# Four 512-token expert items as straight code with the scatter in place, item tables laid over the partitions, one loop left for 64-token items

## The chip, the cores and the metric

The kernel runs on one core of a Trainium2 chip. The metric is the device time of one execution in microseconds; the time of a kernel is the median of several runs. Before the change it is 1185.59 us, the median of 3 runs between 1184.55 and 1185.77.

## What is computed

Three layers follow each other: attention between 8 batches of 512 tokens and 32 state rows, a mixture of 8 experts of which each token takes at most one, and a dense layer with a gated hinge. Cut to what matters:

```python
def _moe_ref(x, w_skip, w_gate, w1, w2):            # x: 4352 x 512
    do_compute = x @ w_skip > 0
    out = x.copy()
    xc = x[do_compute]
    logits = xc @ w_gate
    e_idx = np.argmax(logits, axis=1)
    gate_w = softmax(logits)[np.arange(len(xc)), e_idx]
    for e in range(8):                               # w1[e]: 512x1024, w2[e]: 1024x512
        y[e_idx == e] = gate_w * (relu(xc[e_idx == e] @ w1[e]) @ w2[e])
    out[do_compute] = xc + y

def _moe2_ref(x, w_in, w_out):                       # 512x2048, 2048x512
    h = x @ w_in
    return (h * np.clip(h + 3.0, 0.0, 6.0) / 6.0) @ w_out
```

With the inputs of the runs 2720 tokens are computed. The experts have 544, 0, 0, 32, 544, 1024, 512 and 64 of them: five full blocks of 512 tokens and four remainders of at most 64. These counts are known only when the kernel runs.

## The kernel before, in words

All matmuls on wide data are made in three passes on a high and a low part of each operand (`PAIRS`); the parts come from a ScalarE cast and a VectorE subtraction (`split`, L799, used by `split1` for w1 and `split2` for w2 of an expert).

**Attention** runs over the 8 batches in an order written out by hand (`STEP` and its variants), leaves its rows in `x_in` and scatters the rows that go to an expert into `xs`, sorted by expert, by indirect transfers of GpSimd (`scat`, L379).

**The plan** (`plan`, L593) turns the counts into tables. An item is a block of 512 rows of one expert (an A item) or one of up to 64 rows (a B item). `items_a` (L634, 24 small VectorE operations) writes `tab_a`: how often the A loop runs, and expert and first row of each A item. `items_b` (L668, 21 operations, six of them on 544 columns: 68 possible items times 8 experts) writes `tab_b` and `lim`, the same for the B items. Everywhere the item lies along the free axis.

**The first A item** (`first`, L947) is straight code, for an expert that has 512 rows early. For f of 0 to 7 it runs `s1a(f)`, 12 matmuls 128x512 into `ph`, and `s2a(f-1)`, 12 matmuls into the four sums `po`. Between them it works off a list in small portions (`some`): the last tokens' routing, the plan, and three **conversions** of the last layer's weights (`kept(1)` to `kept(3)`, NEARLY = 4; one is made within attention). A conversion turns two 512 KB blocks of 8-byte numbers into float parts in nine steps (`Weights.cut`, L1264) and stores them (`keep`, L1341). At f = 7 `turn_and_s2a` (L907) transposes the next item's 512 rows (`turn`, 4 groups of 4 transposes into two PSUM banks of the tag `tr`) between the halves of `s2a(6)`. At the end `out_a` (L918) multiplies the four sums by the gates and adds the rows kept in `xr` (`keep`, L931, ScalarE copies).

**The A loop** (`item_a`, L1009, `For_i` at L1144) then runs four times, since `tab_a` holds the larger of the number of A items left and (16-4)/3 = 4. One pass scatters the rows of the item before (`scatter_a`, L922), computes an A item like `first`, computes one B item between its matmuls (`item_b`, L1076, advanced by `next(small)` at the f in SMALL_AT), makes three conversions (`Convert`), and fetches the next item's weights, rows and high and low parts, in the last pass too. `take_wait` (L940) is a one-column GpSimd operation ahead of each scatter.

**The B loop** (L1162) takes the B items that are left, two at a time; with these inputs there are none, and it is passed over. Each loop ends for all engines together (semaphores and drains that the trace puts down to L1144, L1162 and L1851). After it, at L1171 to L1176, come the last A item's four scatters, the reading back of four converted blocks (`again`, `again2`) and their preparation (`W.early`).

**The last layer** (`ffn`, L1358) begins with `fetch(0, True)` and `fetch(2, True)`, four loads of 256 KB of `x_in` on SyncE's queue, which wait for the scatters; the 16 transposes of L1413 and the first matmuls of `stage_a` (L1482) follow. SyncE issues nearly all transfers, in program order.

## Time and profile before

| what | us |
|---|---|
| median of 3 runs | 1185.59 |
| the profiled execution | 1177.61 |
| its span, first to last instruction | 1175.9 |
| TensorE busy in the span | 1110.4 (94%) |
| VectorE busy | 848.4 (72%) |
| ScalarE busy | 499.3 (42%) |
| GpSimd busy | 110.6 (9%) |
| from the first matmul of the last layer to the end | 732.2 |

The profile is of one execution. The span counts the instructions; 1.71 us lie around it. A row of the timeline gives start, length, engine, line, operation, what it writes and reads, and in brackets how long the engine had stood idle and what ended that. Matmuls are pipelined, so consecutive rows overlap by some tenths of a us: 12 matmuls follow each other every 2.80 us though a row reads 2.96. TensorE's granted clock is given as a share of its full 2.4 GHz.

### The profile page before, as it was taken

The numbers are of one execution on the slowest core, as the hardware profiler recorded it, in microseconds if no ns is written. First come the engines' busy times: TensorE is split into PE (matmuls) and PEld (weight loads), VectorE is DVE, ScalarE is ACT, GpSimd is POOL, SyncE is SP. The second block draws the span as 40 slices with busy tenths as digits, with TensorE's granted clock in tenths as the row PEclk, the third lists the DMA queues.
The fourth block names the chain that finished last, engine by engine and source line by source line (L and its number), as shares of the span: only waits on it lengthen the run. The fifth ranks groups of instructions, "written<-read, shape, count | busy, mean of one in ns | idle before, by whom it ended". The sixth has DMA issues, their size and how long they took to land.

```text
span 1175.9 us, 17522 instructions
## 1 busy us (share of the span) xinstructions
PE 1110.4 (94%) x5991; PEld 920.5 (78%) x5991; DVE 848.4 (72%) x1659; ACT 499.3 (42%) x954; POOL 110.6 (9%) x167
## 2 busy tenths in 40 slices
PE   7898979999999919999999999999999999999998
PEld 4555756676767617888998989999889999899997
DVE  6879896666766635686788768876887778876776
ACT  7786443444444414454433343334333343334331
POOL 5466301020201010000000000000000000000000
PEclk9899998999999968999999999999999999999999
DMA  6875888787878746984554256416552454334532
GB/s 199 288 260 200 297 296 300 259 294 265 312 254 305 257 173 256 350 319 175 178 198 152 109 187 212 155 43 226 204 177 86 178 177 173 135 116 164 195 134 90
DMA packets 93080, 245.39 MB, mean 209 GB/s; under 512 B 13744, under 2 KB 43056, under 8 KB 87376
## 3 DMA queue, kind: packets, MB, share of 16 engines
q1 hardware_dynamic: 88496, 233.28, 56.6%
q0 software_dynamic: 4512, 11.17, 2.5%
q8 instruction: 42, 0.69, 0.2%
q14 instruction: 30, 0.25, 0.1%
HBM read 184.75 MB, written 63.22 MB: 211 GB/s over the span
## 4 chain that ended last, share of the span: by engine, by line
PE 61%; DMA 1%; DVE 1%; ACT 0%; issue 0%; POOL 0%; POOLq 0%; SPq 0%; ACTq 0%
PE o L1636 28%; PE b L1584 24%; PE o L1502 4%; PE b L1482 4%; PE o L1413 1%; DMA x_in_dram<-xr,toks 1%; DMA raw<-x_in_dram 0%; ACT g L1306 0%; PE b L1413 0%; DVE cv L1427 0%; POOL x_in_dram L765 0%; DVE g L1307 0%; DVE c L1598 0%; DVE cv L1598 0%; POOL seen L942 0%
## 5 line engine op out<-in xcount | busy, mean ns | idle before, releaser
L1636 PE MATMUL o<-wo,g 128*128 128x512 f32 x1440 | 334.3, 390 | 0.0
L1636 PEld LDWEIGHTS o<-wo,g 128*128 128x128 f32 x1440 | 269.7, 188 | 54.7
L1584 PE MATMUL b<-xc,wc 128*128 128x384 f32 x1680 | 299.6, 335 | 1.6 <-ACT c L1608 1.6
L1584 PEld LDWEIGHTS b<-xc,wc 128*128 128x128 f32 x1680 | 292.2, 188 | 4.0 <-ACT c L1608 1.9
L1307 DVE TENSOR_TENSOR g<-cv,g 128x384 fp32r<-128x384 f32 x160 | 89.3, 558 | 92.8 <-ACT g L1306 92.8
L1306 ACT CAST g<-cv 128x384 fp32r<-128x384 f32 x160 | 82.2, 514 | 157.1 <-DVE cv L1427 157.1
L902 PE MATMUL po<-w2p,hT 128*128 128x512 f32 x480 | 123.1, 403 | 0.0
L890 PE MATMUL ph<-xTa,w1p 128*128 128x512 f32 x480 | 120.3, 401 | 1.1 <-ACT w1p L801 0.8
L902 PEld LDWEIGHTS po<-w2p,hT 128*128 128x128 f32 x480 | 88.3, 190 | 31.3 <-issue 5.5
L1426 ACT ACTIVATE cv<-cv,three 128x384 f32<-128x384 f32 x80 | 49.2, 615 | 143.4 <-DVE cv L1598 135.8
L890 PEld LDWEIGHTS ph<-xTa,w1p 128*128 128x128 f32 x480 | 90.6, 190 | 23.5 <-ACT w1p L801 1.2
L1598 DVE TENSOR_TENSOR c<-b,c 128x384 f32<-128x384 f32 x160 | 87.1, 551 | 16.8 <-PE b L1584 16.4
L1645 DVE SCALAR_TENSOR_TENSOR hl<-o,hl 128x512 f32<-128x512 f32 x140 | 92.7, 683 | 2.1 <-PE o L1636 2.0
L895 DVE SCALAR_TENSOR_TENSOR hT<-ph,hT 128x512 fp32r<-128x512 f32 x40 | 27.5, 689 | 48.7 <-ACT hT L894 48.5
L1426 ACT ACTIVATE cv<-c,three 128x384 f32<-128x384 f32 x80 | 49.2, 614 | 15.0 <-DVE g L1307 15.0
L1598 DVE TENSOR_TENSOR cv<-b,cv 128x384 f32<-128x384 f32 x80 | 44.3, 554 | 14.6 <-PE b L1584 13.4
L894 ACT ACTIVATE hT<-ph 128x512 fp32r<-128x512 f32 x40 | 23.8, 596 | 70.3 <-PE ph L890 64.4
L279 PE MATMUL pxr<-BD,AT 128*128 128x265 f32 x128 | 40.9, 435 | 10.5 <-DVE AT L242 5.2
L1427 DVE SCALAR_TENSOR_TENSOR cv<-cv,c 128x384 f32<-128x384 f32 x80 | 44.1, 552 | 5.8 <-ACT cv L1426 4.8
L1645 DVE SCALAR_TENSOR_TENSOR acc<-o,acc 128x512 f32<-128x512 f32 x70 | 44.8, 681 | 1.3 <-PE o L1636 1.3
L1427 DVE SCALAR_TENSOR_TENSOR cv<-cv,cv 128x384 f32<-128x384 f32 x80 | 43.9, 549 | 0.0
L1608 ACT COPY c<-b 128x384 f32<-128x384 f32 x40 | 19.2, 481 | 55.1 <-PE b L1584 54.9
(294 smaller groups left out, 1302.7 us busy)
## 6 DMA issues: line engine op xcount, KB each, us to landing
wc<-wc SPq DMA_DIRECT2D x36, 1792.0 KB, 6.8
wo<-wo SPq DMA_DIRECT2D x37, 1024.0 KB, 4.9
raw<-in_moe_w_dram SPq DMA_DIRECT2D x48, 512.0 KB, 10.6
spare<-in_moe_w_dram SPq DMA_DIRECT2D x35, 512.0 KB, 4.9
raw<-in_moe_w_in_dram SPq DMA_DIRECT2D x16, 512.0 KB, 6.7
raw<-in_moe_w_out_dram SPq DMA_DIRECT2D x16, 512.0 KB, 5.4
x_in_dram<-XR SPq DMA_DIRECT2D x8, 1024.0 KB
wo<-hl SPq DMA_DIRECT2D x16, 512.0 KB, 7.7
```

What stands on the lines that cost most here:

```text
L890: nc.tensor.matmul(ph, lhsT=w1p[a][:, f, kk, :], rhs=xTa[b][:, kk, :], start=(n == 0), stop=(n == 11))
L902: nc.tensor.matmul(po[c], lhsT=hp[f][a][:, P * c:P * c + P], rhs=w2p[b][:, f, :], start=(f == 0 and n == 0), stop=(f == NF - 1 and n == 2),)
L1306: nc.scalar.copy(hi, src)
L1307: nc.vector.tensor_tensor(lo, src, hi.bitcast(F32), op=ALU.subtract)
L1426: nc.scalar.activation(gg, h, AF.Relu, bias=k["three"])
L1427: nc.vector.scalar_tensor_tensor(gg, gg, 6.0, h, op0=ALU.min, op1=ALU.mult)
L1482: nc.tensor.matmul(ph, lhsT=w1(f, a, kk), rhs=xt[b][:, kk, :], start=(n == 0), stop=(n == 11))
L1502: nc.tensor.matmul(pos[c], lhsT=gg[a][:, P * c:P * c + P], rhs=w2(f, b), start=(f == 0 and n == 0), stop=(f == NFF - 1 and n == 2),)
L1584: nc.tensor.matmul(t, lhsT=w[:, s:s + P], rhs=XC[m // NP][:, x, b, kk, :], start=(i == 0), stop=(i == 5))
L1598: v.tensor_tensor(c, t, u, op=ALU.add)
L1636: nc.tensor.matmul(po, lhsT=gs[f][a][:, o:o + P], rhs=w[:, DM * (2 * f + b):DM * (2 * f + b) + DM], start=(q == 0), stop=(q == 5),)
L1645: nc.vector.scalar_tensor_tensor(dst, po, 1.0 / 6.0, dst, op0=ALU.mult, op1=ALU.add)
```

## The change

The four A items that always ran become straight code, NA = 4, in `for i in range(1, NA + 1)`; full blocks beyond them would be cut into B items. `end_a` takes the place of `turn_and_s2a` for the last two f, of `out_a`, `scatter_a` and `keep`: it ends the sums one by one, multiplies each into the row tile itself and scatters it at once. Two row tiles alternate (`xn`). The last A item fetches, splits and transposes nothing for a next one. Of the last layer's weights two instead of four blocks are converted by the end of `first` (NEARLY = 2); the four items make 3, 3, 3 and 5 conversions in a steady trickle (`convert`), each block loaded during the one before it. SMALL_AT now counts half steps, before and after `s2a`. The plan has the item on the partition: 26 small operations, then three transposes and four VectorE operations (`second`), which run at the end of `first`. The four loads of `x_in` for the last layer are issued after the A items and again in each pass of the B loop.

```diff
-NA = B * TB // 512 + 2
-NB = 8 * NE + 4
+NA = 4
+NSMALL = B * TB // 64 + NE + 2
...
+    n, end, c2, r, nb = (new(nm, [NE]) for nm in ("n", "end", "c2", "r", "nb"))
+    t, m = new("t", [NE, 8]), new("m", [NE + 1, NE])
+    ends, G, w, Z, red = k["ends"], k["G"], new("w", [3, NE]), new("Z", [5, NE]), new("red", [5])
...
+        lambda: v.tensor_scalar(Z[:, 0:2], both, k["item"], None, op0=ALU.is_le),
+        lambda: v.tensor_tensor(w, G[:, :, 1:], G[:, :, 0:NE], op=ALU.subtract),
+        lambda: v.tensor_tensor(Z[:, 2:4], Z[:, 0:2], w[:, 0:2], op=ALU.mult),
+        lambda: v.tensor_tensor(Z[:, 4], Z[:, 1], w[:, 2], op=ALU.mult),
+        lambda: v.tensor_reduce(red, Z, axis=AX.X, op=ALU.add),
+        lambda: v.tensor_scalar(tab[:, 0:2], red[:, 0:2], 7.0, None, op0=ALU.min),
+        lambda: v.tensor_tensor(red[:, 2:5], red[:, 2:5], G[:, :, 0], op=ALU.add),
+        lambda: v.tensor_scalar(tab[:, 2:4], red[:, 2:4], float(NSLOT), None, op0=ALU.min),
+        lambda: v.tensor_scalar(red[:, 4:5], red[:, 4:5], k["item_q"], None, op0=ALU.subtract),
...
+    def second():
+        pt = k["turned"]()
+        vals = [red[:, 4:5], red[:, 1:2], red[:, 3:4]]
+        lim, tb = k["lim"], k["tab_b"]
+        def turn(i):
+            nc.tensor.transpose(pt[:, i, :], vals[i].to_broadcast([P, P]), k["ident"])
+        return [
+            lambda: [turn(i) for i in range(3)],
+            lambda: v.tensor_copy(lim, pt[:, 0, 0:NSMALL]),
+            lambda: v.tensor_scalar(tb[:, 0, :], pt[0:1, 1, 0:NSMALL], 7.0, None, op0=ALU.min),
+            lambda: v.tensor_scalar(tb[:, 1, :], pt[0:1, 2, 0:NSMALL], float(NSLOT), None, op0=ALU.min),
+            lambda: v.tensor_scalar(k["nb"], eb[0:1, 8:9], float(NA), None, op0=ALU.max),
+        ]
...
-        def turn_and_s2a(po, f):
-            if f < NF - 2:
-                return s2a(po, f)
-            self.turn(0)
-            self.turn(1)
-            s2a(po, f, (0, 1))
-            self.turn(2)
-            s2a(po, f, (2, 3))
-            self.turn(3)
-        def out_a(po):
-            for c in range(4):
-                gated(xr[:, c, 0:DM], po[c], xr[:, c])
-        def scatter_a():
-            for c in range(4):
-                take_wait(xr[:, c])
-                i = self.scatter(xr[:, c, 0:DM], toks[:, c:c + 1])
-                tc.declare_no_dep(i, group="xo", reason="rows of different tokens")
-                tc.add_to_no_dep_group("xo", i)
+        def end_a(po, i, last):
+            x, tok = xn[i % 2], toks[:, 4 * (i % 2):4 * (i % 2) + 4]
+            nc.vector.tensor_copy(tok, x[:, :, DM + 1])
+            if last:
+                s2a(po, NF - 2, (0,))
+            else:
+                self.turn(0, (i + 1) % 2)
+                self.turn(1, (i + 1) % 2)
+                s2a(po, NF - 2, (0, 1))
+                self.turn(2, (i + 1) % 2)
+                s2a(po, NF - 2, (2, 3))
+                self.turn(3, (i + 1) % 2)
+            for c in range(4):
+                if last and c < 3:
+                    s2a(po, NF - 2, (c + 1,))
+                s2a(po, NF - 1, (c,))
+                gated(x[:, c, 0:DM], po[c], x[:, c])
+                take_wait(x[:, c])
+                ins = self.scatter(x[:, c, 0:DM], tok[:, c:c + 1])
+                tc.declare_no_dep(ins, group="xo", reason="rows of different tokens")
+                tc.add_to_no_dep_group("xo", ins)
...
+        def convert():
+            todo = list(range(NEARLY, NFF))
+            raw = {todo[0]: self.W.load(todo[0])}
+            for i, f in enumerate(todo):
+                parts, steps = self.W.cut(raw.pop(f))
+                for n, step in enumerate(steps):
+                    step()
+                    if n == 4 and i + 1 < len(todo):
+                        raw[todo[i + 1]] = self.W.load(todo[i + 1])
+                    if n == len(steps) - 1:
+                        self.W.keep(f, parts)
+                    yield
...
-                    self.fetchx(row_a(0))
+                    self.fetchx(row_a(0), xn[1])
...
-                if f >= 1:
-                    turn_and_s2a(po, f - 1)
+                if f == 6:
+                    fetch_b(row_b(0), xb[0])
+                    b0 = expert_b(0)
+                    for c in range(3):
+                        fetch_w(b0, c, chunks[c])
+                if 1 <= f < NF - 1:
+                    s2a(po, f - 1)
                 if f >= 5:
                     split1(2 * f - 10)
                     split1(2 * f - 9)
-            s2a(po, NF - 1)
             some(999)
+            for step in k["tables"]():
+                step()
+            end_a(po, 0, False)
             split1(6)
             split1(7)
-            out_a(po)
...
+        def item_a(i, conv):
+            more = i < NA
+            if more:
+                en, rn = expert_a(i), row_a(i)
+            small = item_b(i - 1, chunks, h32, xb[0], x32[0], hs, yb[0], 0, 1 if more else 0)
+            if more:
+                for f in range(0, NF, 2):
+                    self.fetch1(en, f)
+            po = accs()
+            steps = 9 * CONVERTED[i - 1]
+            done = 0
+            for f in range(NF):
+                if f == 0:
+                    next(small)
+                split2(f)
+                if f % 2 and more:
+                    self.fetch2(en, f - 1)
+                s1a(f)
+                for _ in range(SMALL_AT.count(2 * f)):
+                    next(small)
+                if f == 5 and more:
+                    self.fetchx(rn, xn[(i + 1) % 2])
+                while done < steps * (f + 1) // (NF - 1) and done < steps:
+                    next(conv)
+                    done += 1
+                if 1 <= f < NF - 1:
+                    s2a(po, f - 1)
+                for _ in range(SMALL_AT.count(2 * f + 1)):
+                    next(small)
+                if more and f >= 1:
+                    split1(f - 1)
+            if not more:
+                for f in range(4):
+                    self.W.again(f, self.W.room(f // 2))
+                for f in range(2):
+                    self.W.again2(f)
+            end_a(po, i, not more)
+            if more:
+                split1(NF - 1)
...
-        na = nc.values_load(tab_a[0:1, 0:1], min_val=0, max_val=B * TB // 512)
-        nb = nc.values_load(tab_b[0:1, 0:1], min_val=0, max_val=8 * NE)
-        fetch_b(row_b(0), xb[0])
-        e0 = expert_b(0)
-        for c in range(3):
-            fetch_w(e0, c, chunks[c])
-        with tc.For_i(0, na, 1, iteration_sync="reg_based") as i:
-            item_a(i)
+        nb = nc.values_load(k["nb"][0:1, 0:1], min_val=0, max_val=NSMALL)
+        conv = convert()
+        for i in range(1, NA + 1):
+            item_a(i, conv)
+        self.W.early()
+        self.W.x_first(self.x_in)
...
-        with tc.For_i(na, nb, 2, iteration_sync="reg_based") as i:
+        with tc.For_i(NA, nb, 2, iteration_sync="reg_based") as i:
             for u in range(2):
...
-        scatter_a()
-        for f in range(4):
-            self.W.again(f, self.W.room(f // 2))
-        for f in range(2):
-            self.W.again2(f)
-        self.W.early()
+            self.W.fetch_first(self.x_in)
...
-NEARLY = 4
-NCONV = 3
-LOAD_AT = (0, 0, 3)
-CONV_AT = (1, 3, 5)
-STORE_AT = (3, 5, 7)
-SMALL_AT = (2, 2, 3, 4, 5, 5, 6, 6, 7)
+NEARLY = 2
+CONVERTED = (3, 3, 3, 5)
+SMALL_AT = (2, 4, 5, 7, 9, 11, 12, 13, 14)
...
+    def x_first(self, x_in):
+        self.x0 = [self.scratch(0).bitcast(F32).rearrange("p (c f) -> p c f", c=2) for _ in range(2)]
+        self.fetch_first(x_in)
+    def fetch_first(self, x_in):
+        rows = x_in[0:S].rearrange("(p c) f -> p c f", c=4)
+        for c in range(4):
+            self.tc.nc.sync.dma_start(self.x0[c // 2][:, c % 2], rows[:, c])
...
-    fetch(0, True)
-    fetch(2, True)
+    xw[0], xw[2] = W.x0
```

Where it moves instructions, three places. **VectorE at the end of the first A item**: `w1p`, `w2p` are parts of weights, `hT` of the hidden layer, `xTa` of the transposed rows, `xr`/`xn` the row tiles. Before:

```order
L679 TENSOR_REDUCE tb<-room 128x68
L685 TENSOR_TENSOR spare<-room,ws 128x544
L686 TENSOR_REDUCE lim<-spare 128x68
L687 TENSOR_TENSOR room<-room,w 128x544
L688 TENSOR_REDUCE pr<-room 128x68
L802 TENSOR_TENSOR w1p_1888<-raw_0_97,w1p_1887 128x512 x2
L802 TENSOR_TENSOR w2p_1890<-raw_2029,w2p_1889 128x512
L895 SCALAR_TENSOR_TENSOR hT<-ph,hT 128x512
L802 TENSOR_TENSOR xTa_1747<-ptx,xTa_1746 128x4x128 x4
L802 TENSOR_TENSOR w1p_1888<-raw_1_98,w1p_1887 128x512 x4
L938 SCALAR_TENSOR_TENSOR xr<-po_1946,xr 128x512
```

and with the change:

```order
L762 TENSOR_TENSOR w2p_1896<-raw_2029,w2p_1895 128x512
L854 SCALAR_TENSOR_TENSOR hT<-ph,hT 128x512
L762 TENSOR_TENSOR w1p_1894<-raw_1_98,w1p_1893 128x512 x2
L656 COPY lim<-ptt 128x78
L657 TENSOR_SCALAR tab_b<-ptt 1x78
L658 TENSOR_SCALAR tab_b<-ptt 1x78
L659 TENSOR_SCALAR nb<-ends 1x1
L869 CAST toks<-xn 128x4
L762 TENSOR_TENSOR xTa_1753<-ptx,xTa_1752 128x4x128 x4
L891 SCALAR_TENSOR_TENSOR xn<-po_1952,xn 128x512
```

The wide table operations are gone from between the parts of the weights; four narrow ones that read a PSUM bank of the tag `tr` (`ptt`) stand between `hT` of f = 7 and the row parts `xTa`. **TensorE at the same place**, with the change:

```order
L652 MATMUL ptt<-ident,red 128x128 x3
L768 MATMUL ptx<-ident,xr 128x128 x4
L768 MATMUL ptx<-ident,xr 128x128 x4
```

Ahead of the row transposes, which stood there alone before, three table transposes take one of the two `tr` banks. **SyncE at the end of the A items**, before, from the end of the A loop:

```order
L1144 COMPARE_AND_BRANCH
L1144 UNCONDITIONAL_BRANCH
L1162 COMPARE_AND_BRANCH
L1162 UNCONDITIONAL_BRANCH
L1350 DMA cv_3210<-w 128x512
L1355 DMA hl<-wo 128x1024 x2
L1395 DMA raw_3263<-x_in_dram 128x512 x2
L1395 DMA raw_3266<-x_in_dram 128x512 x2
L1350 DMA wf<-w 128x512
```

and with the change:

```order
L1312 DMA cv_4231<-w 128x512
L1317 DMA hl<-wo 128x1024 x2
L1213 DMA raw_4303<-x_in_dram 128x512 x2
L1213 DMA raw_4304<-x_in_dram 128x512 x2
L1112 COMPARE_AND_BRANCH
L1112 UNCONDITIONAL_BRANCH
L1312 DMA wf<-w 128x512
```

One loop's branches are gone; the other's now stand behind the four loads of `x_in` instead of ahead of the scatters that these wait for.

## Rows read from the trace of the kernel before

**Rows 1.** Windows: stretch, length; busy PE, PEld, DVE, ACT, POOL; clock; DMA share; GB/s.

```profile
125.79:184.52 58.73, 49.35 (x221) 38.53 (x220) 50.97 (x127) 25.84 (x48) 8.64 (x10) 0.94 0.77 276
184.52:243.48 58.96, 57.91 (x263) 41.98 (x263) 37.05 (x64) 24.39 (x44) 6.01 (x10) 0.97 0.83 280
243.48:300.82 57.34, 56.29 (x263) 40.80 (x262) 37.79 (x65) 24.30 (x44) 6.05 (x10) 1.00 0.83 282
...
415.68:443.70 28.02, 3.79 (x16) 2.99 (x16) 8.59 (x16) 4.71 (x8) 5.49 (x8) 0.54 0.53 185
443.70:1175.90 732.20, 726.10 (x3624) 647.23 (x3624) 538.93 (x1006) 278.51 (x512) 0.00 (x0) 1.00 0.48 175
```

**Rows 2.** Timeline of TensorE at the end of the first A item.

```profile
160.04 2.96 PE L902 MATMUL po<-w2p,hT 128*128 128x512 f32 x12
163.78 0.73 PE L890 MATMUL ph<-xTa,w1p 128*128 128x512 f32 x2 [0.79 <-ACT w1p L801]
...
167.26 1.03 PE L808 MATMUL ptx<-ident,xn 128*128 128x128 f32 x8
...
176.09 1.11 PE L808 MATMUL ptx<-ident,xn 128*128 128x128 f32 x4 [6.39 <-DVE xTa L802]
...
184.52 0.41 PE L1051 MATMUL ptx<-ident,xb 128*128 128x128 f32 x2 [1.87 <-DVE xr L938]
184.75 7.36 PE L890 MATMUL ph<-xTa,w1p 128*128 128x512 f32 x24
```

**Rows 3.** Timeline of VectorE in the same place: first and last table operation, rows after.

```profile
163.97 0.23 DVE L674 TENSOR_SCALAR eb<-end 128x8 f32<-128x8 f32 x1
...
175.21 0.23 DVE L699 TENSOR_TENSOR lim<-lim,tb 128x68 f32<-128x68 f32 x1
175.35 1.28 DVE L802 TENSOR_TENSOR xTa<-ptx,xTa 128x512 fp32r<-128x512 f32 x2
```

**Rows 4.** Windows of the tile `cv` alone: busy time of VectorE and ScalarE, three conversions.

```profile
125.79:184.52 58.73, 16.69 (x27) 1.82 (x3) 0.94 0.77 276
```

**Rows 5.** Timeline of TensorE in the A loop: end of the last pass, one wait within.

```profile
392.16 1.08 PE L1117 MATMUL pob<-spare 128*64 128x256 f32 x8 [0.79 <-ACT spare L1052]
...
407.62 0.66 PE L808 MATMUL ptx<-ident,xn 128*128 128x128 f32 x4
408.54 0.66 PE L808 MATMUL ptx<-ident,xn 128*128 128x128 f32 x4 [0.26 <-DVE xTb L1123]
408.95 1.65 PE L902 MATMUL po<-w2p,hT 128*128 128x512 f32 x6
...
412.28 0.60 PE L808 MATMUL ptx<-ident,xn 128*128 128x128 f32 x4
412.64 3.04 PE L902 MATMUL po<-w2p,hT 128*128 128x512 f32 x12
```

**Rows 6.** DMA issues by tile: count, KB each, median us from issue to landing.

```profile
raw<-in_moe_w_dram SPq DMA_DIRECT2D x48, 512.0 KB, 10.6
...
raw<-in_moe_w_out_dram SPq DMA_DIRECT2D x16, 512.0 KB, 5.4
```

**Rows 7.** Timeline from the A loop's end to the last layer, VectorE and GpSimd.

```profile
415.35 2.72 DVE L938 SCALAR_TENSOR_TENSOR xr<-po,xr 128x512 f32<-128x512 f32 x4
...
424.21 0.18 POOL L942 TENSOR_TENSOR seen<-xr 128x1 f32<-128x1 f32 x1 [13.85 <-DMA x_in_dram<-xr,toks]
425.08 1.00 POOL L765 DMA_INDIRECT x_in_dram<-xr,toks  x1 [0.69 <-issue]
```

**Rows 8.** Queue instructions around the passed-over loop: count, ns min/median/max, first and last start.

```profile
L1162 PEldq COMPARE_BRANCH  x2: 73/1706/3340, 419.8 to 420.0; - x2
L1851 SPq EVENT_SEMAPHORE  x2: 17/17/17, 418.8 to 423.9; - x2
```

**Rows 9.** The chain that ended last, in order of time: start, length, what.

```profile
429.73 6.24 DMA x_in_dram<-xr,toks
...
439.24 3.81 PE o L1413 x16
```

More of the change, by code (lines that the diff above doesn't have):

```diff
@@ L586, with plan @@
 NXS = NSLOT + 640
-NA = B * TB // 512 + 2
-NB = 8 * NE + 4
+NA = 4
+NSMALL = B * TB // 64 + NE + 2
 Q = 64
-def plan(tc, sp, c, early, k, spare):
+ROUND = 1.5 * 2.0 ** 23
+def plan(tc, sp, c, early, k):
     nc = tc.nc
@@ L632, in plan @@
-    tab = k["tab_a"]
-    rows, js = new("rows", [NA])[0:1], new("js", [NA])
-    items_a = [
+    n, end, c2, r, nb = (new(nm, [NE]) for nm in ("n", "end", "c2", "r", "nb"))
+    t, m = new("t", [NE, 8]), new("m", [NE + 1, NE])
+    ends, G, w, Z, red = k["ends"], k["G"], new("w", [3, NE]), new("Z", [5, NE]), new("red", [5])
+    ea, eb = ends[:, 0:9], ends[:, 10:19]
+    tab = k["tab"]
+    both = ends[:, 1:19].rearrange("p (i e) -> p i e", i=2)[:, :, 0:NE]
+    first = [
         lambda: v.scalar_tensor_tensor(c2, early, -512.0, c, op0=ALU.mult, op1=ALU.add),
@@ L636, in plan @@
         lambda: v.tensor_tensor(t, over(c2, 8), under(k["i512"], NE), op=ALU.is_ge),
-        lambda: v.tensor_reduce(n[:, 0:8], t, axis=AX.X, op=ALU.add),
-        lambda: v.scalar_tensor_tensor(r, n[:, 0:8], -512.0, c2, op0=ALU.mult, op1=ALU.add),
-        lambda: v.tensor_tensor(t, over(r, 8), under(k["iq"], NE), op=ALU.is_gt),
-        lambda: v.tensor_reduce(n[:, 8:16], t, axis=AX.X, op=ALU.add),
-        lambda: v.tensor_tensor(m, under(n, 16), k["low16"], op=ALU.mult),
-        lambda: v.tensor_reduce(end, m, axis=AX.X, op=ALU.add),
@@ L645, in plan @@
-        lambda: v.tensor_scalar(js, k["iota"][:, 0:NA], end[:, 7:8], None, op0=ALU.min),
-        lambda: v.tensor_tensor(ps, over(js, 16), under(end, NA), op=ALU.is_ge),
-        lambda: v.scalar_tensor_tensor(base, early, 512.0, k["base"], op0=ALU.mult, op1=ALU.add),
-        lambda: v.tensor_reduce(ta[:, 0, :], ps, axis=AX.X, op=ALU.add),
-        lambda: v.scalar_tensor_tensor(g[:, 1:8], end[:, 0:7], -512.0, base[:, 1:], op0=ALU.mult, op1=ALU.add),
-        lambda: v.scalar_tensor_tensor(ta[:, 0, :], ps[:, :, 7], -8.0, ta[:, 0, :], op0=ALU.mult, op1=ALU.add),
@@ new lines, in plan @@
+        lambda: v.tensor_reduce(n, t, axis=AX.X, op=ALU.add),
+        lambda: v.tensor_tensor(m[:, 0:NE], under(n, NE), k["low"][:, 0:NE], op=ALU.mult),
+        lambda: v.tensor_reduce(end, m[:, 0:NE], axis=AX.X, op=ALU.add),
+        lambda: v.tensor_scalar(ea[:, 1:], end, float(NA), None, op0=ALU.min),
+        lambda: v.scalar_tensor_tensor(G[:, 0, 0:NE], early, 512.0, k["base_a"], op0=ALU.mult, op1=ALU.add),
+        lambda: v.tensor_tensor(n, ea[:, 1:], ea[:, 0:NE], op=ALU.subtract),
+        lambda: v.scalar_tensor_tensor(G[:, 0], ea, -512.0, G[:, 0], op0=ALU.mult, op1=ALU.add),
@@ L700, in items_b @@
         ]
-    return items_a, items_b
+    return first, second
 class Experts:
@@ L782, in loadx @@
         row = self.value(self.tab_e, 1, NSLOT + P)
-        self.xn = self.rows("xn", "X")
-        self.tc.add_to_no_dep_group("xa", self.fetchx(row).ins)
+        self.xn = [self.rows("xn", "X")]
+        self.tc.add_to_no_dep_group("xa", self.fetchx(row, self.xn[0]).ins)
     def room(self):
@@ L818, in run @@
         nc = tc.nc
[L819 removed]
+        tab, tab_b = k["tab"], k["tab_b"]
         split, trx = self.split, self.trx
@@ L1080, in item_b @@
                 en, rn = expert_b(j + 1), row_b(j + 1)
-            else:
+            elif more is None:
                 for c in range(n):
@@ L1091, in item_b @@
             turned32(x, xt, 2 * P)
-            drop, tok = drops[:, u:u + 1], toks[:, 4 + u:5 + u]
+            drop, tok = drops[:, u:u + 1], toks[:, 8 + u:9 + u]
             v = nc.vector
@@ L1388, in ffn, with fetch @@
     xw = {}
-    def fetch(c0, apart=False):
+    def fetch(c0):
         t = W.scratch(0).bitcast(F32).rearrange("p (c f) -> p c f", c=2)
         for p, rows in rows_of(x_in, c0):
-            if apart:
-                for c in range(2):
-                    nc.sync.dma_start(t[p, c], rows[:, c])
-            else:
-                nc.sync.dma_start(t[p], rows)
+            nc.sync.dma_start(t[p], rows)
         xw[c0] = t
@@ L1806, in items @@
         def items():
-            first, *rest = plan(tc, pp3, count, ex.early, k, W.spare)
-            after.extend(rest)
+            k["turned"] = lambda: pools[2].tile([P, 4, P], F32, tag="tr", name="ptt")
+            first, k["tables"] = plan(tc, pp3, count, ex.early, k)
             return first
```

172 lines of the change are left out of this document (44 added, 128 removed).

## The prediction

> **What bounds the kernel now.** I read the windows by stage first, since the share of the whole span mixes stages with different limits. From the first matmul of the last layer on, TensorE works 726.1 of 732.2 us [rows 1]; nothing of that stage is touched, so those 732.2 us stay. Within the A loop a pass takes 57.34 us, of which TensorE works 56.29: it is the bound there, and only its own work or its waits can be shortened. Two stretches are different. In the first A item it works 49.35 of 58.73 us, and between its last matmul of the A loop and the first of the last layer, 28.02 us, it works 3.79. These are the places where the change can bring something.
>
> The timeline of TensorE then shows where the first item loses. `s2a(5)` starts at 160.04 and twelve matmuls run 2.80 us, so `s1a(7)` could start at 162.84; it starts at 163.78 on a ScalarE copy of w1, and the transposes follow at 167.26 where 165.64 was possible. There it stands 6.39 us for `xTa`, and 1.87 us at the loop's entry [rows 2]. VectorE says why: 21 table operations of `items_b` lie between 163.97 and 175.21, mixed with weight parts, and the `xTa` part that frees the transposes' bank comes only at 175.35 [rows 3]. The stage's three conversions take 16.69 us of VectorE besides [rows 4].
>
> The chain and the queues tell the end. The last sums are done on VectorE from 415.35 on, the scatters begin at 425.08 [rows 7], the last one's transfer runs 6.24 us from 429.73, and the last layer's transposes start at 439.24 [rows 9]. Ahead of the scatters both loops are left: all engines meet at 418.8 and, past the empty B loop, again at 423.9, and TensorE's sequencer alone stands 3.34 us in a branch [rows 8].
>
> **The change part by part.** Sums are made against the profiled execution, 1177.61 us, and the median of the runs is 7.98 us above it. I take this distance to stay.
>
> *The first item.* Two of three conversions leave it, 11.1 of 16.69 us of VectorE [rows 4], and 21 table operations become four on a narrow bank. With that ScalarE's copies come in time and `s1a(7)` ends at 165.64: a gain of 1.6. From there to the next item's `s1a(0)` it was 167.26 to 184.75, so 17.5. The same work in a loop pass: 407.62 to the end of twelve matmuls begun at 412.64, so 7.8 with the 0.26 wait, and 0.2 for the next transposes [rows 2, 5]; 8.0. New are three table transposes, 0.3, and a wait: they take one of two `tr` banks, and the second row group needs it back. In VectorE's order four narrow reads of it stand behind `hT` of f = 7 and two weight parts. After `s1a(7)` that is 0.6 for ScalarE (1.82 for three, [rows 4]), 0.7 for `hT` (2.72 for four of that size, [rows 7]), 1.2 for the parts (1.28 for two, [rows 3]) and three narrow reads at 0.2, 3.1 in all; TensorE is there at 0.8, after the tables' and the first group's transposes, so it waits 2.3. After the 1.87 wait of before, 24 matmuls took 7.36 instead of 5.6 plus tail [rows 2], and this pass was 1.62 longer than the next at a granted clock of 0.97 instead of 1.00 [rows 1]; half of 2.4 GHz for some of them. I charge 1.5 for the same after the new wait. 8.0 + 0.3 + 2.3 + 1.5 = 12.1, a gain of 5.4. Together **7.0**. Bounds: 10.8 if neither wait nor slow clock comes; 3 if the next expert's w1 lands late (landing has medians of 10.6 and 5.4 us [rows 6]; it is asked for at f = 3, and ScalarE stands at its copies at f = 5). I stay near the middle, as the `hT(6)` behind those copies is wanted only after `s1a(7)`.
>
> The 26 operations of the first part of the plan stay where 24 stood, under matmuls that ran gapless up to 160.04 [rows 2]; nothing. If that cover went, they would cost some 6 us (26 times 0.23, [rows 3]).
>
> *The loop's entry.* The 1.62 us of the first pass go with the 1.87 wait that caused them (the new wait is charged above): **1.6**.
>
> *Small items.* The two steps that met in one f, transposing the hidden rows and using them, are now a whole f apart; the 0.79 wait [rows 5] goes in all four items: **3.2**. Bounds 0 and 3.2.
>
> *The last item* drops sixteen transposes: 407.62 to 408.95 is 1.33, and each of the other two groups moves the next matmuls by 0.36 [rows 5]: **2.0**. The useless weight loads and parts it drops were beside TensorE's work: nothing. Five conversions there are 28 us of VectorE [rows 4] where it loses eight w1 parts; per f that is 28 / 7 = 4.0 and two parts at 0.7, 5.4, against 55 / 8 = 6.9 us of TensorE, which covers it. If the cover went, each conversion's load could show.
>
> *The first conversion's load* is a new wait. It is issued on SyncE behind the w1 loads of the item, the last of which waits for `split1(7)`: about 4.9 us into the item. With 5.4 [rows 6] it lands at 10.3, and three steps of 0.62 [rows 4], then `split2(1)` and `hT(1)`, 0.7 each, stand behind it on VectorE, so 13.6 to 14. TensorE wants them for `s2a(1)` at 13.2. **-0.7**; bounds 0, and -4.7 with a landing of 10.6. Later loads have a whole conversion's time. Each store is now right behind its last step on SyncE, so the fetches queue behind that wait; they are not wanted before the next f.
>
> *The end.* The scatters of three quarters go out under matmuls; the last follows its sum. From TensorE's end: a quarter of 2.72 us, 0.7; 0.87 from the one-column operation to the scatter [rows 7]; 6.24 to landing [rows 9]; then four loads. Before, their first transposes stood 3.3 us behind the landing and the sixteen took 3.81, paced by them, so the last load was in after some 5.8. Now the order matters: SyncE enters the B loop behind these loads and waits for them there, and TensorE may go on only past the loop's end. SyncE's own way from 418.8 to 423.9 was 5.1 [rows 8]. Then 4.46 from transposes to the first matmuls (439.24 to 443.70). 0.7 + 0.9 + 6.2 + 5.8 + 5.1 + 4.5 = 23.2 against 28.0: **4.8**. Bounds: 8.7 if SyncE passes in the 1.2 us that remain of the 5.1 when the branch and the moves ahead of it cost nothing; 1.5 if TensorE's 3.34 us branch comes after it and not beside it. `again` and `W.early` run while the scatters travel, as before.
>
> The Trainium skill (DMA: Bandwidth & Descriptors, Anatomy of one DMA — SWDGE (gpsimd) path) fits GpSimd's transfers as 2.0 us plus bytes over 436 GB/s; for 256 KB that is an estimate of 2.6 us. The row's 6.24 disagrees, and the measurement decides; by the page the time would be 3.6 us less, 1164.1.
>
> Sum: 7.0 + 1.6 + 3.2 + 2.0 - 0.7 + 4.8 = 17.9 us. 1177.61 - 17.9 = 1159.7 for a profiled execution; 1185.59 - 17.9 = **1167.7** for the median.
>
> **The rivals.** *Waits eat most of it.* Weights land late in the first item (3 instead of 7.0), the first conversion's load costs 4.7, the B loop's end costs 8.4 instead of 5.1 (1.5 instead of 4.8): 3 + 1.6 + 3.2 + 2.0 - 4.7 + 1.5 = 6.6, so 1179.0. For it: the transfer engines were full in the first item's second half, and the loop is still there, now behind the loads. Transfers are busy 0.77 of that stage and 0.83 of a pass [rows 1]. Against: two conversions less are also two pairs of stores less just there.
>
> *The tables are as late as before.* If the transposes wait for the plan's values or the narrow reads stand behind weights that are late, the 5.4 and 1.6 vanish: 10.9 are left, 1174.7. Against it: the 26 operations are done by f = 1.
>
> *Slower: the code itself arrives late.* A loop's body is run again and again; straight code is new each time. An item is 526 TensorE instructions [rows 1]; if they came late twice an item, eight times in all, and each time cost what the branch did, 3.34 us [rows 8], that is 27 us, and the median 1185.59 - 17.9 + 27 = 1194.7. It decides from about six such stalls on (17.9 / 3.34). Against it: 3624 matmuls of the last layer are straight code with 6 us idle in all [rows 1]. The Trainium skill (Runtime: NRT & Kernel Launch, Instruction fetch mechanics) says that the next block is fetched while one runs, mostly hidden, and that a taken branch breaks this; by it the rival costs nothing, and the rows of the last layer agree.
>
> **How the numbers follow.** About 2.4 us, 0.2%, is what a measurement of this kernel can tell from no change. The forecast has 0.68, the late tables 0.1, the waits 0.1; a twentieth is for no change, where that last one has its worse end. Slower gets 0.07. So faster 0.88, same 0.05, slower 0.07. The range goes from all terms at their better ends, 10.8 + 1.6 + 3.2 + 2.0 + 8.7 = 26.3, so 1159.3, to 1177.0, where most of the rival of waits is in.
>
> **What would show it.** Right: TensorE without the 6.39 and 1.87 waits, a wait of 2 to 3 us ahead of the second row group, `s1a(0)` of the second item near 177; items of 56.5 us, the last near 55; the last scatter issued within 2 us of TensorE's end, and 23 us from that end to L1482's new counterpart. Wrong: TensorE idle with no releaser inside items (code), w1 copies of ScalarE waiting past 165, VectorE waiting at the first conversion beyond 14 us into the second item, or the transposes of the last layer starting more than 6 us behind their loads.

## The result, and the profile after

| | before | changed |
|---|---|---|
| median of the runs, same session (us) | 1185.07 | 1167.32 |
| lowest to highest (us) | 1183.11 to 1185.77 | 1163.63 to 1169.27 |
| ratio | | 0.9849, 95% interval 0.982 to 0.9879 |
| profiled execution, its span (us) | 1177.61, 1175.9 | 1166.02, 1164.3 |

The changed kernel is faster by 17.75 us; 17.9 were forecast, and 1167.3 stands against 1167.7. The two profiled executions differ by 11.6 only, since before's lay 8 us under its median. So the stages are compared twice: here with the rows shown ahead, and below with a second pair of profiles from one session.

The windows by stage of the changed kernel: stretch, length, busy TensorE, weight loads, VectorE, ScalarE, GpSimd, granted clock, DMA share, GB/s. The stretches are the first item, the four items behind it (the third of these, 57.33 us and so like the second, is left out), the end and the last layer.

```profile
130.79:184.62 53.83, 51.47 (x222) 41.05 (x223) 33.70 (x93) 20.47 (x38) 7.14 (x8) 0.92 0.65 228
184.62:245.94 61.32, 58.80 (x264) 41.41 (x262) 38.05 (x67) 22.11 (x40) 6.83 (x10) 0.97 0.77 271
245.94:303.28 57.34, 57.08 (x264) 40.38 (x262) 37.51 (x66) 22.21 (x40) 7.48 (x10) 1.00 0.81 283
...
360.61:415.92 55.31, 55.31 (x247) 38.62 (x245) 42.27 (x73) 20.66 (x37) 8.83 (x13) 1.00 0.65 219
415.92:434.17 18.25, 3.38 (x18) 3.17 (x17) 6.73 (x13) 3.38 (x5) 3.60 (x5) 0.63 0.66 220
434.17:1164.30 730.13, 723.96 (x3624) 645.73 (x3624) 539.05 (x1007) 278.51 (x512) 0.00 (x0) 1.00 0.48 175
```

Against [rows 1] the first item is 4.9 us shorter, the second 2.4 *longer*, the third unchanged (57.34 to 57.34), and the end 9.8 shorter (18.25 for 28.02). The first item starts 5.0 us later than the 125.79 of before, and its first twelve matmuls take 5.46 us at a granted clock of 0.50, against 3.03 at 1.00 before.

TensorE at the first item's end, which answers to [rows 2]: the 6.39 us stop is gone and one of 2.36 stands there, where 2.3 was forecast.

```profile
172.84 0.49 PE L652 MATMUL ptt<-ident,red 128*128 128x128 f32 x3
...
176.13 0.63 PE L768 MATMUL ptx<-ident,xr 128*128 128x128 f32 x4 [2.36 <-DVE toks L869]
176.51 2.43 PE L861 MATMUL po<-w2p,hT 128*128 128x512 f32 x6
...
184.76 5.87 PE L849 MATMUL ph<-xTa,w1p 128*128 128x512 f32 x24
```

VectorE in the same place answers to [rows 3]. The two weight parts, then the four table reads, then the token column: the order that the prediction counted out.

```profile
174.27 1.28 DVE L762 TENSOR_TENSOR w1p<-raw,w1p 128x512 fp32r<-128x512 f32 x2
175.47 0.23 DVE L656 COPY lim<-ptt 128x78 f32<-128x78 f32 x1
...
175.97 0.15 DVE L869 CAST toks<-xn 128x4 int32<-128x4 f32 x1
```

The loss in the second item, in the timelines of SyncE, VectorE, ScalarE and TensorE, in this order. The two loads of its first conversion are issued at 190.05 and 190.49, behind the last weights of the next expert; VectorE stands 8.58 us for the second of them, the `hT` that waits behind it comes at 200.03, and TensorE stops 2.26 us. Then twelve matmuls take 4.72 us instead of 3.06, at a granted clock of 0.63.

```profile
190.05 0.39 SPq L1219 DMA_DIRECT2D raw<-in_moe_w_in_dram  x1
...
197.76 0.43 DVE L1240 TENSOR_SCALAR cv<-raw 128x512 int32<-128x512 int32 x1 [8.58 <-DMA raw<-in_moe_w_out_dram]
...
200.03 0.60 ACT L853 ACTIVATE hT<-ph 128x512 fp32r<-128x512 f32 x1
...
200.68 4.72 PE L861 MATMUL po<-w2p,hT 128*128 128x512 f32 x12 [2.26 <-ACT hT L853]
```

The end, which answers to [rows 7, 9]: SyncE's loads of converted parts, the last scatter on GpSimd, SyncE's loads of the last layer's rows, which wait for its landing, and TensorE.

```profile
407.98 3.97 SPq L1312 DMA_DIRECT2D cv<-w  x4
...
418.88 1.03 POOL L725 DMA_INDIRECT x_in_dram<-xn,toks  x1 [0.16 <-issue]
...
422.17 1.74 SPq L1213 DMA_DIRECT2D raw<-x_in_dram  x4
...
430.12 3.37 PE L1371 MATMUL o<-ident,raw 128*128 128x128 f32 x16 [14.20 <-PEq L1808]
```

Queue instructions at the empty loop in the same stretch answer to [rows 8] (count, ns, first and last start). SyncE comes to it at 424.0, its last semaphore is at 429.0, and all engines are let go at 429.9.

```profile
L1112 SPq EVENT_SEMAPHORE  x17: 17/17/28, 424.0 to 429.0; - x17
...
L1808 PEldq EVENT_SEMAPHORE  x1: 51/51/51, 429.9 to 429.9; - x1
```

### The profile page after: what moved, and what is told of

It reads as the page before. It is cut to its first block, busy times and chain, and to the rows that moved or that the text cites. A ratio compares the mean times of both kernels' runs of the same rounds, so it can differ in the third digit from the quotient of the medians.

```text
span 1164.3 us, 16315 instructions
## 1 busy us (share of the span) xinstructions
PE 1112.9 (96%) x5978; PEld 920.0 (79%) x5978; DVE 834.1 (72%) x1632; ACT 482.0 (41%) x922; POOL 114.8 (10%) x170
## 4 chain that ended last, share of the span: by engine, by line
PE 61%; DVE 1%; ACT 0%; issue 0%; ACTq 0%
PE o L1594 28%; PE b L1542 24%; PE o L1460 4%; PE b L1440 4%; PE o L1371 1%; ACT g L1268 0%; PE b L1371 0%; DVE cv L1385 0%; DVE g L1269 0%; DVE c L1556 0%; DVE xt L1269 0%; DVE cv L1556 0%; DVE gg L1385 0%; ACT gg L1384 0%; DVE wc L1269 0%
## 5 line engine op out<-in xcount | busy, mean ns | idle before, releaser
L849 PE MATMUL ph<-xTa,w1p 128*128 128x512 f32 x480 | 122.8, 407 | 0.0
L1250 ACT ACTIVATE raw<-raw 128x512 f32<-128x512 f32 x32 | 22.0, 689 | 51.5 <-DVE cv L1246 48.8
```

The source lines that it names most:

```text
L849: nc.tensor.matmul(ph, lhsT=w1p[a][:, f, kk, :], rhs=xTa[b][:, kk, :], start=(n == 0), stop=(n == 11))
```

## Experiments

**The same two kernels again.** No edit. This asks what of the stages is the spread of executions.

> The kernel before, once more, for its stages. The time that stood beside the change's gain in single profiles was 1177.6, while its median is 1185.6. Theory (the profile of before was a lucky one): the stretch up to the first matmul of the first item, 125.8 there, comes out 3 to 8 us longer this time, and the stretches behind it (58.7, 59.0, 57.3, 28.0 and 732.2 us) stay within 0.5 us each. Rival (the spread lies in the experts or the FFN): one of the later stretches moves by over 2 us.

> The changed kernel, once more, for its stages. Theory (the 5.0 us later start of the first item, 130.8 against 125.8, is the spread of the attention stage and not the change): the start moves by over 1 us from 130.8, and the 3.0 us stop at the router's last matmuls (line 414) and the half clock behind it are not the same. Rival (the change's code delays it): the start stands at 130.8 within 0.5 us with the same stop. Under both, the stretches behind it stay: 53.8, 61.3, 57.3, 57.3, 55.3, 18.3 and 730.1, each within 0.7 us.

Measured: 1183.08 and 1168.03. The timeline of TensorE of the kernel before, second profile:

```profile
130.42 0.85 PE L414 MATMUL prl<-W,sxt 128*96 128x9 f32 x8 [2.31 <-issue]
131.12 3.05 PE L890 MATMUL ph<-xTa,w1p 128*128 128x512 f32 x12
...
191.17 0.41 PE L1051 MATMUL ptx<-ident,xb 128*128 128x128 f32 x2 [1.49 <-DVEq L1144]
...
417.88 3.04 PE L902 MATMUL po<-w2p,hT 128*128 128x512 f32 x12
...
449.56 5.05 PE L1482 MATMUL b<-xt,wc 128*128 128x512 f32 x12 [0.68 <-ACT xt L1306]
```

And of the changed kernel, second profile:

```profile
130.36 4.26 PE L849 MATMUL ph<-xTa,w1p 128*128 128x512 f32 x12
...
183.27 0.38 PE L1003 MATMUL ptx<-ident,xb 128*128 128x128 f32 x2
...
409.06 5.88 PE L861 MATMUL po<-w2p,hT 128*128 128x512 f32 x24
...
434.27 5.38 PE L1440 MATMUL b<-xt,wc 128*128 128x512 f32 x12 [0.68 <-ACT xt L1268]
```

The kernel before starts its first item at 131.12 this time, 5.3 later than in its first profile, behind a stop of 2.31 us at line 414. So the stop and the late start are not the change's. The changed kernel alone would not have told: its start, 130.36, stayed within 0.5 us of 130.79, as the rival had it, with the stop at 2.33 instead of 3.02. The stages behind also move more than I allowed: before's first two items took 60.05 and 57.52 us instead of 58.7 and 59.0, and the changed kernel's first item, end and last layer 52.91, 19.33 and 732.0 instead of 53.8, 18.3 and 730.1. The last of these is half clock in the first matmuls: the twelve that open the last layer take 5.38 us here, at a granted clock of 0.55 from 434.3 to 439.6, where the first profile has 1.00 from 434.2 to 439.0. The stage lengths of this pair, in us:

| stage | before | changed | gain |
|---|---|---|---|
| up to the first item | 131.12 | 130.36 | 0.8 |
| first item | 60.05 | 52.91 | 7.1 |
| second item | 57.52 | 61.68 | -4.2 |
| third and fourth | 114.71 | 114.67 | 0.0 |
| fifth item | 57.52 | 55.32 | 2.2 |
| TensorE's end to the last layer | 28.64 | 19.33 | 9.3 |
| last layer | 731.74 | 732.03 | -0.3 |
| span | 1181.3 | 1166.3 | 15.0 |

**Old places of the small items' pieces.**

```diff
-SMALL_AT = (2, 4, 5, 7, 9, 11, 12, 13, 14)
+SMALL_AT = (4, 4, 6, 8, 10, 10, 12, 12, 14)
```

> The changed kernel with the pieces of the small item in the old places, two of them in pairs. Theory (a pair costs the wait of 0.79 us and saves one switch between matmul groups, which costs about as much): the stretch of the second and third looped item stays within 0.3 us of 57.3, with the wait of 0.7 to 0.8 us back in it; the whole time is that of the changed kernel within 0.3%. Rival (the places matter, term C): 0.8 us longer in each of the four items, 3.2 in all.

Measured: 1166.96 us, ratio 0.9848 (0.9831 to 0.9865). TensorE's timeline in the third item: the wait is back, and the item, 243.11 to 300.58, takes 57.47 us.

```profile
243.11 0.38 PE L1003 MATMUL ptx<-ident,xb 128*128 128x128 f32 x2
...
254.65 1.94 PE L1053 MATMUL phb<-spare,xTb 128*64 128x512 f32 x8
...
277.18 1.08 PE L1069 MATMUL pob<-spare 128*64 128x256 f32 x8 [0.79 <-ACT spare L1004]
...
300.58 0.38 PE L1003 MATMUL ptx<-ident,xb 128*128 128x128 f32 x2
```

The difference is 0.13 us an item, 0.5 in four, not 0.79 and 3.2. What the new places save as a wait they give back in switches. From start to start two pieces together take 1.86 us (254.65 to 256.51) and in the changed kernel 1.01 each; a group of twelve takes 2.80 alone, 2.90 behind a piece and 3.00 between two. The new order has eight such pieces among the groups where the old one has six. The theory holds.

**The conversion's load earlier.** `NEARLY` is the number of the first conversion that the items behind the first take.

```diff
                     for c in range(3):
                         fetch_w(b0, c, chunks[c])
+                    self.ahead = self.W.load(NEARLY)
...
-            raw = {todo[0]: self.W.load(todo[0])}
+            raw = {todo[0]: self.ahead}
```

> The changed kernel with the load of the first looped conversion issued in the first item, ahead of the next expert's first weights, instead of behind them. Theory (the load landed at 197.7 and VectorE's queue stood 8.6 us for it, so the activation of the next hidden block came late and TensorE stopped 2.26 us and then ran 1.7 us longer at half clock): the stop in the second item goes, its stretch falls from 61.3 to 57.3, whole time 4 us less than the changed kernel. Rival (it is put off, not removed: the earlier load delays the next expert's weights, which are issued behind it): another stop of 2 us or more appears in the first or second item, gain under 1.5 us.

Measured: 1161.74 us, ratio 0.9811 (0.9777 to 0.9845). SyncE issues the load at 172.40, and TensorE's timeline shows the same twelve matmuls without a stop:

```profile
172.40 0.39 SPq L1220 DMA_DIRECT2D raw<-in_moe_w_in_dram  x1
...
183.39 0.38 PE L1004 MATMUL ptx<-ident,xb 128*128 128x128 f32 x2
...
197.08 3.07 PE L861 MATMUL po<-w2p,hT 128*128 128x512 f32 x12
...
240.68 0.38 PE L1004 MATMUL ptx<-ident,xb 128*128 128x128 f32 x2
```

The item takes 57.29 us, 4.4 less than the 61.68 of the same session, and no new stop appears. By time it is 5.2 us under the version with the old places and 6.3 under the one execution of the changed kernel. So the whole loss of that item is this load's position in the queue. The stage shows it; by time alone the runs (1159.75 to 1167.81) overlap those of the version with the old places (1165.78 to 1169.06).

**The loop left out.**

```diff
-        with tc.For_i(NA, nb, 2, iteration_sync="reg_based") as i:
...
-            self.W.fetch_first(self.x_in)
```

> The changed kernel with the loop over further 64-token items left out: items beyond the fourth are not computed, of which these inputs have none. In the changed kernel SyncE asks for the rows of the last layer at 422.2, comes to the loop at 424.0 and is out of it at 429.9, and TensorE's transposes start at 430.1. Theory (SyncE waits inside the loop's entry for these loads, then takes its branch, and all engines wait for it): without the loop the transposes begin as the rows land, 1 to 3 us sooner after TensorE's end than the 14.2 us now, and the time falls by about that. Rival (the landing alone decides, the loop's end lies beside it): 14.2 stays within 0.5 us.

Measured: 1157.38 us, one execution, in a session in which the kernel before took 1177.82. GpSimd, SyncE and TensorE at the end:

```profile
412.61 1.01 POOL L725 DMA_INDIRECT x_in_dram<-xn,toks  x1 [0.16 <-issue]
...
415.82 1.74 SPq L1203 DMA_DIRECT2D raw<-x_in_dram  x4
...
419.15 1.94 PE L1361 MATMUL o<-ident,raw 128*128 128x128 f32 x8 [9.20 <-DMA raw<-x_in_dram]
...
423.91 4.76 PE L1430 MATMUL b<-xt,wc 128*128 128x512 f32 x12 [0.68 <-ACT xt L1258]
```

TensorE ends at 409.95; the stop falls from 14.20 to 9.20, more than the 1 to 3 us expected, and the last layer starts 13.96 us after that end instead of 18.25. The transposes now begin 3.33 us after the loads are asked for, before the last has landed (the second eight still wait 0.18 us for a load, at 421.26); with the loop it was 7.95 (422.17 to 430.12), and 7.6 to 8.4 in the seven other profiles that have the loop and no added loads. The empty loop thus costs 4.2 to 5.1 us in its new place, by the traces. The time of one execution can't show it: the changed kernel has no run beside it, and where the kernel before took 1176.16 the runs of the changed kernel took 1156.19 to 1163.07. Why is in part open: all loads must be in before SyncE leaves it, and its branch and the meeting of the engines come on top, and this run doesn't part the two. The rows narrow it: SyncE's way from its first semaphore at the loop to the release took 5.9 us (424.0 to 429.9), and 5.1 before (418.8 to 423.9 [rows 8]), where these loads had not been asked for, so waiting for them seems to add little. Asking for these rows only behind the loop wasn't tried.

**More loads beside the scatters.**

```diff
             end_a(po, i, not more)
+            if not more:
+                for f in range(8):
+                    nc.sync.dma_start(self.room1[f // 4][:, f % 4], self.W.w32[f])
```

> The changed kernel with eight more loads of 256 KB each, whose data nothing uses, on SyncE's queue right behind the six that fetch converted parts at the end of the last 512-token item. Before the change the six loads ran beside the last scatters, whose landing took 6.24 us; now they are issued at 408 and the last scatter lands 3.3 us after its start. Theory (the loads in the transfer engines made the landing of before long): with more loads under way the last scatter lands 5 to 7 us after its start, and the stretch from TensorE's end to the last layer's first matmul grows from 18.3 by 2 us or more. Rival (the landing differs for another reason): landing 3.0 to 3.6 us, the stretch grows by under 1 us.

Measured: 1160.96 us, one execution. The last scatter, the added loads, and the loads that wait for the scatter, on GpSimd and SyncE:

```profile
411.86 1.03 POOL L725 DMA_INDIRECT x_in_dram<-xn,toks  x1 [0.16 <-issue]
...
405.90 8.47 SPq L998 DMA_DIRECT2D raw<-w  x8
418.79 1.95 SPq L1216 DMA_DIRECT2D raw<-x_in_dram  x4
```

From the scatter's start to the loads it is 6.93 us, against 3.29 in the changed kernel (418.88 to 422.17) and 3.21 without the loop (412.61 to 415.82); the kernel before had 6.38 (429.73 to 436.11, 6.24 of it the transfer [rows 9]). The two short ones are not the whole range: the changed kernel's second profile has 4.48, from a scatter at 417.90 to these loads:

```profile
422.38 1.74 SPq L1213 DMA_DIRECT2D raw<-x_in_dram  x4
```

All nine profiles of the changed kernel and its versions without added loads lie between 3.2 and 4.5; why they differ is open. Before's second profile has 6.36. SyncE had issued the added loads by 414.4 (405.90 + 8.47), so what it then waited for was the scatter; its waits name `x_in_dram<-xn` as well. The stretch from TensorE's end at 408.90 to the last layer at 429.09 is 20.2 us, 1.9 more than the 18.25 of the first profile but only 0.9 more than the 19.33 of the second, so the stretch doesn't decide. The landing does, and the theory holds for it: loads in flight made it 1.5 to 2.2 times as long. This fits what the change did, which has the converted parts fetched at 408, ahead of the scatters, where before they were fetched at 424, beside them; moving these loads alone wasn't tried.

**Two conversions back into the first item.**

```diff
-NEARLY = 2
-CONVERTED = (3, 3, 3, 5)
+NEARLY = 4
+CONVERTED = (3, 3, 3, 3)
```

> The changed kernel with two of the sixteen conversions put back into the first item, where the kernel before had them, so that the looped items have three each. Theory (the conversions taken out of the first item are what brings the weights' copies in time, and the shorter tables are what shortens the end of the item): the copies are late again, 1 to 2 us of waits ahead of s1a(7), and the wait at the second row group grows from 2.4 to 4 us or more; first item 3 to 6 us longer than 53. The fifth item stays at 55.3. Rival (the tables alone made the gain): the first item stays within 1 us of 53.

Measured: 1160.09 us, one execution. TensorE at the first item's end:

```profile
126.91 4.57 PE L849 MATMUL ph<-xTa,w1p 128*128 128x512 f32 x12
...
166.15 2.60 PE L849 MATMUL ph<-xTa,w1p 128*128 128x512 f32 x10 [0.19 <-DVE w1p L762]
...
172.68 0.63 PE L768 MATMUL ptx<-ident,xr 128*128 128x128 f32 x4 [3.16 <-DVE toks L869]
...
179.64 0.38 PE L1003 MATMUL ptx<-ident,xb 128*128 128x128 f32 x2
```

The weights' copies cost 0.19 us, not 1 to 2, and the wait at the second row group grew by 0.8 to 3.16. The first item is 52.73 us. By the length of the item the rival holds, but the clock hides a part of what the conversions do. The first twelve matmuls took 4.57 us here (granted clock 0.60 from 127.0 to 131.3), against 3.03 before, so that, counted from `s1a(0)`, TensorE came 1.5 us later to the copies; and the six matmuls behind the 3.16 wait ran at full clock (1.64 us). Counted from `s1a(0)`, the matmuls that wait for VectorE's part of w1 start at 39.24 us and the transposes at 41.68; before it was 39.05 and 41.47. So with the conversions back the copies are as late as they were. Without them and with a start at full clock, as before, the transposes come at 39.62 us, in the version with more loads, whose first item is that of the changed kernel:

```profile
126.47 3.05 PE L849 MATMUL ph<-xTa,w1p 128*128 128x512 f32 x12
...
166.09 0.49 PE L652 MATMUL ptt<-ident,red 128*128 128x128 f32 x3
```

The two conversions thus seem to account for most of the 1.85 us gained up to the transposes, though no run has them back behind a start at full clock, and for 0.8 us of the wait behind. The rest of that wait's gain, from 6.39 to 3.16 us, is not theirs; the shorter tables are its likely cause, and these were not undone by themselves.

**Both edits: load earlier, tables at f = 5.** To the edit of the conversion's load is added:

```diff
                 if f == 5:
                     self.fetch1(e0, 6)
+                    for step in k["tables"]():
+                        step()
...
             some(999)
-            for step in k["tables"]():
-                step()
             end_a(po, 0, False)
```

> The changed kernel with two edits: the load of the first looped conversion issued in the first item (that edit alone gave 1161.7), and the steps that turn the tables moved from the first item's end to f = 5. Theory (the wait of 2.4 us at the second row group and the half clock behind it come from the tables' hold on one of the two transpose banks): both go, the first item takes 49 to 51 us instead of 53, whole time 1157 to 1160. Rival (another wait takes its place, as the next wait of the turned rows on the split of the first group): the wait at the second row group stays over 1.5 us, whole time 1161 to 1163.

> The changed kernel a third time, beside the version with both edits, on one chip. Theory (the start of the first item moves with the session and its chip, not with the kernel): where the kernel before takes 1183 to 1187, the first item starts at 130 to 131 behind a stop of 2.3 us at line 414, where it takes 1176 to 1180, at 126 to 127 behind 0.8; in both the ratio to before is 0.982 to 0.988. Rival (it moves with the kernel's code): the start does not follow the time of the kernel before.

> The version with both edits again. Theory: 7 to 9 us under the changed kernel of the same session (4.0 from the conversion's load, 2.4 from the tables' wait, 1.5 from half clock), ratio to before 0.975 to 0.981; first item 48 to 50 us, second 57.3. Rival (its 1152 came from an attention stage that was short by luck, with the first item's start at 121.7): 4 to 6 us under the changed kernel.

Measured: 1152.22 us, ratio 0.978 (0.975 to 0.9811); then, with the changed kernel beside it, 1154.75, ratio 0.9824 (0.9793 to 0.9855), against 1159.47, ratio 0.9846 (0.9817 to 0.9874). TensorE's timeline of the second of these profiles:

```profile
125.78 3.05 PE L849 MATMUL ph<-xTa,w1p 128*128 128x512 f32 x12
...
169.17 0.66 PE L768 MATMUL ptx<-ident,xr 128*128 128x128 f32 x4 [1.01 <-DVE xTa L762]
...
174.32 0.38 PE L1004 MATMUL ptx<-ident,xb 128*128 128x128 f32 x2
...
231.66 0.38 PE L1004 MATMUL ptx<-ident,xb 128*128 128x128 f32 x2
```

The transposes of the first two row groups now go at once, and a smaller wait, 1.01 us, takes the place of the 2.37, at the third group. The first item takes 48.54 us where the changed kernel beside it took 52.99 (126.73 to 179.72), the second 57.34 where it took 60.46: 7.6 us by stages. The medians are 4.7 apart, as the rival had it, with runs of each that spread over 6 to 7 us, more than before's 4.5. So this version beats the kernel before. Against the changed kernel the stages show a gain; by time the first ratio, 0.978, lies clear of the changed kernel's, while the second pair of ratios, from one session, has intervals that overlap. How much the time gains, and whether the tables' edit shows in it beside the other, whose ratio was 0.9811, stays open. The third profile of the changed kernel starts its first item at 126.73 behind a 0.79 stop, in a session where the kernel before took 1176.16. So the start follows the session, with one exception: the first profile of the version with both edits starts its first item at 121.68, in the session in which three other versions start theirs between 126.47 and 126.91. What sets it stays open.

## Why the prediction was right, point by point

The total was right, and most of the mechanisms, but that it came out within 0.2 us is luck: errors of size on both sides, the small items and the conversion's load against the end, nearly cancel. Of 17.9 us forecast, the second pair of profiles shows 15.0 and the medians 17.75.

- **First item and loop entry (7.0 + 1.6 = 8.6): 7.1.** The item's end was right: 12.1 us from the end of `s1a(7)` to the next `s1a(0)` were worked out, 11.92 and 11.94 measured, with the 2.3 us wait at the named place (2.36). The 1.6 for `s1a(7)` was right too where like is compared with like: from `s1a(0)` to the transposes it is 41.47 us before and 39.62 with more loads, 41.93 in before's second profile and 40.37 with the old places, so 1.85 and 1.56 less. In all four the first twelve matmuls ran at full clock (3.03 to 3.05 us), and the stop behind them is the same within each pair: none, and 0.58 and 0.59 us. The changed kernel's own two profiles lose most of it to a half clock at the start that before's did not have. The 1.6 for the loop's entry was not always there to be gained: before's second profile has 57.52 us for that pass, against 58.96 in the first.
- **Small items (3.2): 0.** The wait went, as forecast, and the pass stayed at 57.34. The step failed where it took a wait out and priced the new order at nothing: pieces that come singly need more switches between groups of matmuls. So the items took 57.34 us, not the 56.5 named as a sign.
- **Last item (2.0): 2.2.** And the five conversions' cover held: TensorE was busy 55.31 of 55.31 us.
- **First conversion's load (-0.7, bounds 0 and -4.7): -4.2.** The mechanism and the queue of steps behind it were right; the landing was taken from the shorter of two rows, 5.4 us. The two loads were issued at 190.05 and 190.49 and VectorE started on them at 197.76, 7.3 us after the second, and the matmuls behind the stop took 1.7 us more at a granted clock of 0.63, which the term didn't have. The bound of -4.7 doesn't follow from the forecast's own steps: with 10.6 for the landing they end at 18.8 us, 5.6 behind the 13.2.
- **End (4.8, bounds 1.5 and 8.7): 9.3 and 9.8.** Two terms were mis-sized. The landing was taken as 6.2 from a row of before, where loads ran beside it; it was 3.3 and 4.5. Loads and loop, added up as 5.8 + 5.1 = 10.9, took 7.7 (422.17 to 429.9), for they lay beside each other: SyncE's way began when the loads were issued, at 424.0, and took 5.9. Against this the last scatter came 3.0 us after TensorE's end, not 1.6, as the four scatters queued up on GpSimd. The transposes started 7.95 us behind their loads; more than 6 was named as a sign of being wrong, although the forecast's own sum has 10.9 there.
- **The rivals.** Late code did not show: the items have no stop without a releaser, and TensorE is busy 57.08 of 57.34 us. The Trainium skill (Runtime: NRT & Kernel Launch, Instruction fetch mechanics) has straight code fetched ahead; these rows agree. Of the waits that would eat the gain, the conversion's load came at nearly its full price, and the weights' lateness did not.
- **The distance of 7.98 us** between before's profiled execution and its median was taken to stay. Most of it is an early first item, 125.79 against 131.12 in the second profile. The changed kernel's profile lay 1.3 us under its own median, so most of the 6.2 us by which the difference of the profiles (11.6) falls short of that of the medians (17.75) is that start.

## What to carry to other kernels

Price a removed wait together with the order that removes it: a wait of 0.79 us against two more pieces between matmul groups came out even. Put the first load of a chain ahead of fetches that wait for a buffer on the same queue; that one position cost 4 us here and an edit of two lines took it back. A transfer's landing is no constant of the transfer: before it is used in a sum, see in the timeline what else is in the transfer engines then, and will be in the new place.

## What the runs showed of the hardware

- From the start of the last 256 KB scatter to the loads that wait for it, it took 3.2 to 4.5 us in nine profiles in which no loads were issued beside it, and 6.4 to 6.9 in three with 2 MB of loads beside it. The Trainium skill (DMA: Bandwidth & Descriptors, Anatomy of one DMA — SWDGE (gpsimd) path) gives 2.6 by its fit, as an estimate; the undisturbed scatter is nearer to it than the row of before was, but above it in all nine.
- The same stop was followed by half clock in one execution and by full clock in another. Behind the 2.36 us stop at 176.13 the changed kernel's first six matmuls took 2.43 us; its window there has a granted clock of 0.60 (columns as in the first fence):

```profile
176.60:178.90 2.30, 2.30 (x9) 1.72 (x8) 0.80 (x2) 0.59 (x1) 0.00 (x0) 0.60 0.89 338
```

In the version with the old places the stop was 2.37 us, the six took 1.64, and the window has 1.00, the level of 2.4 GHz:

```profile
174.90:176.40 1.50, 1.50 (x10) 1.19 (x8) 0.80 (x2) 0.59 (x1) 0.00 (x0) 1.00 1.02 396
```

So the 1.5 us charged for it in the forecast came in some executions and not in others.
- An empty loop cost 4.2 to 5.1 us at the end of a stage with nothing else to do, by one execution without it.
- The start of the first item moved with the session, 126 to 131 us, in both kernels, between sessions on the same chip too; one profile, of the version with both edits, started at 121.68.
